# A decode attention kernel: transposing half a K tile per instruction, and setup work moved off VectorE

## The chip, the cores and the metric

The kernel runs on one core of a Trainium2 chip. A core has a matrix engine (TensorE, PE in the profile), three engines for elementwise work (VectorE or DVE, ScalarE or ACT, GpSimd or POOL), an engine that issues loads (SyncE or SP) and 16 load engines (DMA) that bring data from memory (HBM) to the on-chip buffer (SBUF). TensorE writes to a second buffer, PSUM. The engines run beside each other and wait for one another through semaphores.

The metric is the time on the device in microseconds (us), as the median of several runs. The profile shows one execution; its span is a little shorter than the time.

## What is computed

For four sequences with one new token each, the kernel adds three things: the input `x`, an attention over a cache, and an MLP mixer. Cut to what matters:

```python
def _A_ref(x, k_cache, v_cache, wq, wo):          # attention over the last W = 2048 positions
    q = (x @ wq).reshape(B, 1, 32, 128)           # 32 query heads, 16 key/value heads
    k = repeat(k_cache[:, :, Sk - W:, :], 2)      # (4, 16, 2048, 128) of K are read, bf16
    v = repeat(v_cache[:, :, Sk - W:, :], 2)      # and as much of V
    p = softmax(q @ k.T * 128 ** -0.5)
    return (p @ v).reshape(B, 1, 4096) @ wo

def _B_ref(x, w1, w2, w3, w4):                    # with one token the first mixing part is zero
    ...
    x1 = x + hs
    return x1 + gelu(layernorm(x1) @ w3) @ w4     # w3: 576 x 4608, w4: 4608 x 576

xn = layernorm(x)
out = x + _A_ref(xn, ...) + _B_ref(xn, ...)
```

Nearly all of the 87 MB that the kernel has to read is K and V: 16 heads, each with 2 MB of K and 2 MB of V for the four sequences. The weights wq, w3, w4 and wo make up the rest. Each value is used for one token only, so there is little arithmetic for each byte.

## The kernel before

The kernel goes through the 16 key/value heads in 16 steps. Step `t` makes the scores of head `t`; beside that, it does the softmax of head `t - 1`, the product with V ("PV") of head `t - 2`, and the rest of heads `t - 3` and `t - 4`. A step has four slices.

K lies in SBUF with positions on the partitions, and the scores need it with the head's 128 dimensions there. VectorE transposes it in blocks of 32 x 32, a quarter of a K tile for each instruction, through a pool of three buffers:

```python
ktp = ctx.enter_context(tc.tile_pool(name="kt", bufs=3))
...
def k_transpose(h, s):
    src = kv_tiles["K", h][:].bitcast(I32)[:, s * SC:(s + 1) * SC, :].rearrange("p c (ib i) -> p ib c i", i=QD)
    kt = ktp.tile([P, 2, SC, QD], I32, tag="kt")
    nc.vector.transpose(out=kt[:], in_=src)
    kts[h, s] = kt

def k_scores(h, s):                    # TensorE: four matmuls for a slice
    kt = kts.pop((h, s))[:].bitcast(BF16)
    for ie in range(4):
        ...
        nc.tensor.matmul(out=S_ps[h][:], lhsT=qz[:, z0:z0 + P], rhs=kt[...], ...)

def sm_max(h):                         # VectorE: the maxima of a head's scores
    nc.vector.reduce_max(out=mx[:], in_=S_ps[h][:], axis=AX.X)
    nc.vector.tensor_scalar(out=dm[:], in0=sel_g[:], scalar1=mx[:, 0:1], ...)

def pv(h, s):                          # TensorE: four matmuls for a slice
    for g in range(NQD):
        c = s * NQD + g
        nc.tensor.matmul(out=O_ps[h][g * QD:(g + 1) * QD], lhsT=PT[h][:, c, :], rhs=vn[:, :, c, :], ...)
```

The helper `part` cuts small tiles from the first buffer of the wo pool. The loop over the steps, in which the order of the instructions is fixed by hand:

```python
k_transpose(0, 0)
for t in range(Hkv):
    hm, hv, hf, hp = t - 1, t - 2, t - 3, t - 4
    for s in range(NSL):                       # NSL = 4
        if s == NSL - 1 and hm >= 0:
            sm_turn(hm)                        # VectorE: transpose of the exponentials
        n = t * NSL + s + 1
        if n < Hkv * NSL:
            k_transpose(*divmod(n, NSL))       # the quarter for the slice that follows
        if s == 0:
            if hm >= 0:
                sm_max(hm)
            if hv >= 0:
                sm_rec(hv)                     # VectorE: reciprocal of the denominator
            if hp >= 0:
                o_pick(hp)                     # VectorE, every fourth head
            if hf >= 0:
                o_scale(hf)                    # ScalarE
            k_mask(t)                          # TensorE
        elif s == 1 and hm >= 0:
            sm_maxT(hm)                        # TensorE
        elif s == 2:
            if hm >= 0:
                sm_sub(hm)                     # TensorE: subtracts the maxima
                sm_exp(hm)                     # ScalarE
            if hf >= 0:
                o_sum(hf)                      # VectorE
        elif s == 3 and hm >= 0:
            sm_den(hm)                         # TensorE
        k_scores(t, s)
        if hv >= 0 and s > 0:
            pv(hv, s - 1)
            if s == NSL - 1:
                pv(hv, s)
        if s == 1:
            ...                                # sm_neg(hm) on VectorE, o_turn(hf), o_proj(hp) on TensorE
        ...                                    # o_spread; in step 7 the MLP: mlp_g, mlp_turn, mlp_act
    pos["free"] += 1                           # the K tile of this step
    if hv >= 0:
        pos["free"] += 1                       # the V tile of head t - 2
    flush_loads()
```

`flush_loads` issues the next loads on one queue, in the order K0, K1, K2, V0, K3, V1, K4, V2 (then w3), K5, V3 and so on, with a piece of wo ahead of V0, V4, V8 and V12, and w4 in six pieces at the end. K and V tiles share six buffers of 2 MB. A load waits until its buffer is free. After the loop, the last two heads are finished, and then TensorE multiplies the MLP's activations with w4, piece by piece, and head 15's last part with wo. The result is the sum of two accumulators in PSUM.

Ahead of the loop stands a setup: two layernorms, selection matrices made from an identity, and the projection with wq. In it, and in the MLP's activation, VectorE does these operations which the change touches:

```python
nc.vector.memset(dup[:], 0.0)                                  # in transposed(), called twice
nc.vector.tensor_copy(out=dup[:, e, e:P:2], in_=...)           # two per call
nc.vector.tensor_copy(out=sel[:, :, :, kb, :], in_=...)        # four
nc.vector.tensor_copy(out=ohT[:], in_=oh_ps[:, 0, :])
nc.vector.tensor_copy(out=sel_jb[:], in_=sel_j[:])
nc.vector.tensor_copy(out=j_row[:], in_=jT_ps[:])
nc.vector.tensor_copy(out=same_j[:]..., in_=...)
nc.vector.tensor_tensor(out=xsum[:], in0=xn_f[:], in1=x_bf[:], op=ALU.add)

def mlp_act():                                                 # once, 128 x 144 values
    nc.vector.tensor_tensor(out=u[:], in0=xs[:], in1=xs[:], op=ALU.mult)
    nc.vector.tensor_scalar(out=u[:], in0=u[:], scalar1=GELU_A, scalar2=1.0, ...)
    nc.vector.tensor_tensor(out=u[:], in0=u[:], in1=xs[:], op=ALU.mult)
    nc.scalar.activation(out=u[:], in_=u[:], func=ACT.Tanh, scale=GELU_C)
    nc.vector.tensor_scalar(out=u[:], in0=u[:], scalar1=0.5, scalar2=0.5, ...)
    nc.vector.tensor_tensor(out=gT[:, :, ROWS], in0=u[:], in1=xs[:], op=ALU.mult)
```

Of the kernel before, what the change touches and what calls it, by code (L numbers as in the profile page):

```python
# [8 lines left out]
ACT = mybir.ActivationFunctionType  # L9
ALU = mybir.AluOpType  # L10
AX = mybir.AxisListType
BF16 = mybir.dt.bfloat16
F32 = mybir.dt.float32
I32 = mybir.dt.int32
# [8 lines left out]
def kernel(  # L23
# [14 lines left out]
    nc = tc.nc  # L38
    P = 128
    B, Sq, D = A_x.shape  # L40
    _, Hkv, Sk, Dh = A_k_cache.shape
# [5 lines left out]
    KJ = 4  # L47
# [5 lines left out]
    NJ = B * rep  # L53
    QD = 32
    NQD = P // QD
    NSL = 4
    SC = NC // NSL
# [7 lines left out]
    GELU_A = 0.044715  # L65
# [11 lines left out]
    kvp = ctx.enter_context(tc.tile_pool(name="kv", bufs=NKV))  # L77
    wp = ctx.enter_context(tc.tile_pool(name="w", bufs=1))
    wop = ctx.enter_context(tc.tile_pool(name="wo", bufs=2))
    ktp = ctx.enter_context(tc.tile_pool(name="kt", bufs=3))  # L80
    ptp = ctx.enter_context(tc.tile_pool(name="pt", bufs=2))
    bigp = ctx.enter_context(tc.tile_pool(name="big", bufs=2))
    const = ctx.enter_context(tc.tile_pool(name="const", bufs=1))
# [9 lines left out]
    kv_tiles = {}  # L93
# [22 lines left out]
    x_bf = part(D, B)  # L116
# [52 lines left out]
    ROWS = slice(NI - 1, NI - 1 + OR, NI)  # L169
    gT = cleared([P, NF, OW], "gT")  # L170
    op = cleared([P, WOR, OW], "op")
# [30 lines left out]

    def transposed(src_bf, T):
        dup = small.tile([B, 2, P], BF16, tag="dup")
        nc.vector.memset(dup[:], 0.0)
        for e in range(2):
            nc.vector.tensor_copy(out=dup[:, e, e:P:2], in_=src_bf[:, KJ * P:D])
        tp = ps_m.tile([P, KJ + 2, B], BF16, tag="m", name="tp")
        for j in range(KJ):
            nc.tensor.transpose(out=tp[:, j, :], in_=src_bf[:, j:KJ * P:KJ], identity=ident_bf[0:B, 0:B])  # L210
        for e in range(2):
            nc.tensor.transpose(out=tp[:, KJ + e, :], in_=dup[:, e, :], identity=ident_bf[0:B, 0:B])
        nc.vector.tensor_copy(out=T[:, :, 0:B], in_=tp[:])

    xn_f = part(2 * D, B).bitcast(F32)
# [3 lines left out]

    kts = {}  # L220

    def k_transpose(h, s):
        src = kv_tiles["K", h][:].bitcast(I32)[:, s * SC:(s + 1) * SC, :].rearrange("p c (ib i) -> p ib c i", i=QD)
        kt = ktp.tile([P, 2, SC, QD], I32, tag="kt")
        nc.vector.transpose(out=kt[:], in_=src)  # L225
        kts[h, s] = kt


    sel = part(4 * P).rearrange("p (i e k x) -> p i e k x", i=2, e=2, k=NQD)
    for kb in range(NQD):  # L230
        nc.vector.tensor_copy(out=sel[:, :, :, kb, :],
                              in_=ident_bf[:].rearrange("p (ib i e) -> p ib e i", ib=2, e=2))
    oh4 = const.tile([P, B], F32)
    nc.vector.reduce_sum(out=oh4[:], in_=ident_f[:].rearrange("p (k b r) -> p b k r", b=B, r=rep), axis=AX.XY)
# [2 lines left out]
    oh_ps = ps_m.tile([B, 2, P], F32, tag="m", name="oh_ps")  # L237
    nc.tensor.transpose(out=oh_ps[:, 0, :], in_=oh4[:], identity=ident_f[:])
    nc.tensor.transpose(out=oh_ps[:, 1, :], in_=ohk[:], identity=ident_f[:])
    ohT = const.tile([B, P], BF16)  # L240
    nc.vector.tensor_copy(out=ohT[:], in_=oh_ps[:, 0, :])
    negbig = const.tile([B, QD], BF16)
    nc.vector.tensor_scalar(out=negbig[:], in0=oh_ps[:, 1, 0:QD], scalar1=-1.0, scalar2=BIG,
                            op0=ALU.add, op1=ALU.mult)

    NG = P // NJ
    sel_j = const.tile([P, NJ], F32)
    nc.vector.reduce_sum(out=sel_j[:], in_=ident_f[:].rearrange("p (g j) -> p j g", j=NJ), axis=AX.X)
    sel_jb = const.tile([P, NJ], BF16)
    nc.vector.tensor_copy(out=sel_jb[:], in_=sel_j[:])  # L250
    sel_g = const.tile([P, NG], BF16)
    with nc.allow_low_precision("zeros and ones"):
        nc.vector.reduce_sum(out=sel_g[:], in_=ident_f[:].rearrange("p (g j) -> p g j", j=NJ), axis=AX.X)
    jT_ps = ps_m.tile([NJ, P], F32, tag="m", name="jT_ps")
    nc.tensor.transpose(out=jT_ps[:], in_=sel_j[:], identity=ident_f[:])
    j_row = const.tile([NJ, P], BF16)
    nc.vector.tensor_copy(out=j_row[:], in_=jT_ps[:])
    same_j = const.tile([P, P], F32)
    nc.vector.tensor_copy(out=same_j[:].rearrange("p (g j) -> p g j", j=NJ),
                          in_=sel_j[:].unsqueeze(1).to_broadcast([P, NG, NJ]))  # L260


# [7 lines left out]
    nc.gpsimd.memset(idz[:], 0.0)  # L270
    nc.gpsimd.tensor_copy(out=idz[:, ROWS], in_=ident_f[0:B, 0:B])
    xsum = xn_f
    nc.vector.tensor_tensor(out=xsum[:], in0=xn_f[:], in1=x_bf[:], op=ALU.add)
    acc_matmuls([(idz[:], xsum)])
    ln2_bf = part(D, B)
    layernorm(None, ln2_bf, xn_bf)
# [25 lines left out]
    for r in range(2):  # L302
        nc.vector.tensor_copy(out=q_bf[:, r],
                              in_=qT_ps[:, r].rearrange("p u (g x) -> p g u x", g=NQD)[:, :, :, 0:B])
    qs_ps = ps_m.tile([P, Hkv, 4, rep, B], F32, tag="m", name="qs_ps")
    for ie in range(4):
        ib, e = divmod(ie, 2)
# [13 lines left out]
    E = {}  # L321
# [5 lines left out]
    def k_mask(h):  # L327
        S_ps[h] = ps_s.tile([P, NW], F32, tag="S", name="S")
        nc.tensor.matmul(out=S_ps[h][:].rearrange("p (c k) -> p c k", k=QD), lhsT=ohT[:],  # L329
                         rhs=negbig[:].unsqueeze(1).to_broadcast([B, SC, QD]),  # L330
                         start=True, stop=False, skip_group_check=True)

    def k_scores(h, s):
        kt = kts.pop((h, s))[:].bitcast(BF16)
        for ie in range(4):
            ib, e = divmod(ie, 2)
            z0 = (h * 4 + ie) * P + ZP - s * NJ
            nc.tensor.matmul(out=S_ps[h][:], lhsT=qz[:, z0:z0 + P],  # L338
                             rhs=kt[:, ib, :, e:2 * QD:2].rearrange("p c k -> p (c k)"),
                             start=False, stop=False, skip_group_check=True)  # L340

    def sm_max(h):
# [18 lines left out]
                         start=False, stop=False, skip_group_check=True)  # L361

    def sm_exp(h):
        E[h] = ptp.tile([P, SC, QD], BF16, tag="e", name="E")
        rs = small.tile([P, 1], F32, tag="rs", bufs=3)
        nc.scalar.activation(out=E[h][:].rearrange("p c k -> p (c k)"), in_=S_ps.pop(h)[:], func=ACT.Exp, scale=scale,  # L366
                             accum_out=rs[:])
        st["rs", h] = rs
# [5 lines left out]
    def sm_den(h):  # L374
        dn = ps_m.tile([P, 1], F32, tag="m", name="dn")
        nc.tensor.matmul(out=dn[:], lhsT=same_j[:], rhs=st.pop(("rs", h))[:], start=True, stop=True)  # L376
        st["dn", h] = dn
# [6 lines left out]
    def pv(h, s):  # L384
        if s == 0:
            O_ps[h] = ps_o.tile([P, NSL, Dh], F32, tag="O", name="O")
        vn = kv_tiles["V", h][:].rearrange("p (s c) d -> p s c d", s=NSL)
        for g in range(NQD):
            c = s * NQD + g
            nc.tensor.matmul(out=O_ps[h][g * QD:(g + 1) * QD], lhsT=PT[h][:, c, :], rhs=vn[:, :, c, :],  # L390
                             start=(s == 0), stop=False, skip_group_check=True)
        if s == NSL - 1:
            PT.pop(h)

    def o_scale(h):
        O_sb[h] = bigp.tile([P, NSL, Dh], F32, tag="big", name="O_sb")
        nc.scalar.activation(out=O_sb[h][:], in_=O_ps.pop(h)[:], func=ACT.Copy, scale=st.pop(("rd", h))[:, 0:1])  # L397
# [77 lines left out]

    def mlp_act():
        u = const.tile([P, NF, B], F32, name="g_u")
        nc.vector.tensor_tensor(out=u[:], in0=xs[:], in1=xs[:], op=ALU.mult)
        nc.vector.tensor_scalar(out=u[:], in0=u[:], scalar1=GELU_A, scalar2=1.0, op0=ALU.mult, op1=ALU.add)
        nc.vector.tensor_tensor(out=u[:], in0=u[:], in1=xs[:], op=ALU.mult)  # L480
        nc.scalar.activation(out=u[:], in_=u[:], func=ACT.Tanh, scale=GELU_C)
        nc.vector.tensor_scalar(out=u[:], in0=u[:], scalar1=0.5, scalar2=0.5, op0=ALU.mult, op1=ALU.add)
        nc.vector.tensor_tensor(out=gT[:, :, ROWS], in0=u[:], in1=xs[:], op=ALU.mult)

    def mlp_out(lo, hi):
        w4 = w_tiles["w4"]
# [29 lines left out]
    for t in range(Hkv):  # L516
        hm, hv, hf, hp = t - 1, t - 2, t - 3, t - 4
        for s in range(NSL):
            if s == NSL - 1 and hm >= 0:
                sm_turn(hm)  # L520
            n = t * NSL + s + 1
            if n < Hkv * NSL:
                k_transpose(*divmod(n, NSL))

            if s == 0:
                if hm >= 0:
                    sm_max(hm)
                if hv >= 0:
                    sm_rec(hv)
                if hp >= 0:  # L530
                    o_pick(hp)
                if hf >= 0:
                    o_scale(hf)
                k_mask(t)
            elif s == 1 and hm >= 0:
                sm_maxT(hm)
            elif s == 2:
                if hm >= 0:
                    sm_sub(hm)
                    sm_exp(hm)  # L540
                if hf >= 0:
                    o_sum(hf)
            elif s == 3 and hm >= 0:
                sm_den(hm)
            k_scores(t, s)
            if hv >= 0 and s > 0:
                pv(hv, s - 1)
                if s == NSL - 1:
                    pv(hv, s)
            if s == 1:  # L550
                if hm >= 0:
                    sm_neg(hm)
                if hf >= 0:
                    o_turn(hf)
                if hp >= 0:
                    o_proj(hp)
            elif s == 3 and hf >= 0:
                o_spread(hf)
            if t == G_AT:
                if s < 3:  # L560
                    mlp_g(s)
                if s > 0:
                    mlp_turn(s - 1)
                if s == NSL - 1:
                    mlp_act()
        pos["free"] += 1
        if hv >= 0:
            pos["free"] += 1
        flush_loads()
# [77 lines left out]
```

## Time and profile before

| what | value |
|---|---|
| time, median of 3 runs | 212.51 us (212.32 to 212.71) |
| span of the profiled execution | 210.7 us |
| bytes read | 87.17 MB on the queue that loads K, V and the weights |
| K transposes on VectorE | 64, 1222 ns each |
| score matmuls on TensorE (`S<-kt,qz`) | 75.1 us busy in all |
| PV matmuls on TensorE (`O<-vn,PT`) | 24.0 us busy in all |
| mean clock granted to TensorE | 0.87 of full speed |

In a page of the profile, the busy time of an engine stands first, then its share of the span and its number of instructions. A row of digits cuts the span into 40 equal slices; a 9 means busy for 90% or more. A group of instructions is given as line, engine, operation, what it writes and reads, and its count; then the busy time and the mean of one in ns; then the engine's idle time just before such instructions, and what ended most of it. In a timeline a line starts with the start and the duration in us; in brackets is the idle time before it with its releaser. The load share of a stretch is the mean busy share of the 16 load engines, and can come out slightly over 1.

### The profile page before, as it was taken

Reading aid. Unit: us, or ns where it says so; the run is one execution under the profiler, and the core shown is the slowest. Engines: PE = TensorE matmul, PEld = TensorE weight load, DVE = VectorE, ACT = ScalarE, POOL = GpSimd, SP = SyncE. Lnnn points to the kernel's source line nnn. Section 1 sums busy time; section 2 is a strip of 40 time slices with the busy share of each in tenths; the row PEclk is TensorE's granted clock in tenths of the full one; section 3 lists DMA queues with packets and bytes.
Section 4 is the critical chain, followed back from the end, with each engine's and each line's share of the span. In section 5 each row is a group of like instructions: output and inputs, shape, how many; then the busy total and the mean of one; then the engine's idle time right before and its main releaser. Section 6 shows DMA issues by size and latency. Waiting matters only on the chain.

```text
span 210.7 us, 2383 instructions
## 1 busy us (share of the span) xinstructions
PE 153.2 (73%) x941; PEld 61.2 (29%) x955; DVE 120.7 (57%) x217; ACT 33.9 (16%) x64; POOL 2.7 (1%) x15
## 2 busy tenths in 40 slices
PE   0288399768660069559997699999885757999585
PEld 0133133223220013123443224334332212343253
DVE  3741889794910094917227867985939481845300
ACT  7602201112020001111122012121120201113200
POOL 4010000000000000000000000000000000000000
PEclk9999669999995558966999759999999965599969
DMA  7999999999999999999999999999999999999990
GB/s 299 398 426 423 439 426 417 428 445 417 487 388 411 447 426 420 429 442 439 414 439 435 417 432 429 442 426 428 428 432 429 422 440 432 423 432 447 397 396 31
DMA packets 6659, 87.32 MB, mean 414 GB/s; under 512 B 748, under 2 KB 1016, under 8 KB 1656
## 3 DMA queue, kind: packets, MB, share of 16 engines
q1 hardware_dynamic: 6640, 87.17, 97.1%
q8 instruction: 7, 0.11, 0.2%
q10 hardware_dynamic: 8, 0.00, 0.1%
q14 instruction: 4, 0.03, 0.0%
HBM read 87.17 MB, written 0.00 MB: 414 GB/s over the span
## 4 chain that ended last, share of the span: by engine, by line
DMA 63%; PE 26%; DVE 7%; issue 2%; ACT 1%; SPq 0%; DVEq 0%
DMA vn<-in_A_v_cache_dram 29%; DMA w_sb<-in_B_w_dram 16%; DMA kn<-in_A_k_cache_dram 12%; PE S L338 8%; DMA wq_sb<-in_A_wq_dram 6%; PE acc L183 4%; DVE kt L225 4%; PE O L390 3%; PE oT L403 2%; PE g_ps L456 2%; PE q_ps L285 2%; PE S L360 1%; PE dn L376 1%; DVE qz L317 1%; PE gT_ps L468 1%
## 5 line engine op out<-in xcount | busy, mean ns | idle before, releaser
L338 PE MATMUL S<-kt,qz 128*128 128x512 bf16 x242 | 75.1, 432 | 24.8 <-DVE kt L225 22.3
L225 DVE STREAM_TRANSPOSE kt<-kn 128x1024 int32<-128x1024 int32 x64 | 76.6, 1222 | 25.7 <-DMA kn<-in_A_k_cache_dram 23.8
L338 PEld LDWEIGHTS <-qz 128*128 128x128 bf16 x256 | 23.7, 109 | 54.9 <-issue 38.5
L390 PE MATMUL O<-vn,PT 128*32 128x512 bf16 x256 | 24.0, 417 | 7.4 <-DMA vn<-in_A_v_cache_dram 7.1
L366 ACT ACTIVATE E<-S 128x512 bf16<-128x512 f32 x16 | 9.5, 597 | 97.4 <-PE S L360 97.4
L372 DVE STREAM_TRANSPOSE PT<-E 128x512 bf16<-128x512 bf16 x16 | 11.4, 710 | 14.0 <-ACT E L366 13.9
L397 ACT ACTIVATE O_sb<-O,rd 128x512 f32<-128x512 f32 x16 | 11.0, 686 | 39.4 <-issue 28.9
L390 PEld LDWEIGHTS <-PT 128*32 128x32 bf16 x256 | 5.9, 95 | 29.6 <-issue 28.9
L413 DVE TENSOR_REDUCE on<-oT 128x8 bf16<-128x128 f32 x16 | 4.5, 283 | 14.4 <-PE oT L403 14.4
L403 PE MATMUL oT<-ident_w,O_sb 128*128 128x128 f32 x64 | 12.4, 324 | 0.3 <-ACT O_sb L397 0.3
L344 DVE TENSOR_REDUCE mx<-S 128x1 f32<-128x512 f32 x16 | 10.6, 660 | 2.0 <-PE S L338 2.0
L351 PE MATMUL mg<-dm,sel_jb 128*8 128x16 bf16 x16 | 2.8, 173 | 9.2 <-DVE dm L346 9.1
L403 PEld LDWEIGHTS oT<-ident_w,O_sb 128*128 128x128 f32 x64 | 7.9, 160 | 5.0 <-issue 4.5
L183 PE MATMUL acc<-w_sb,gT 128*8 128x288 bf16 x38 | 6.6, 342 | 2.4 <-DMA w_sb<-in_B_w_dram 2.4
L183 PE MATMUL acc<-wo_sb,op 128*8 128x288 bf16 x56 | 7.5, 286 | 0.0
L360 PE MATMUL S<-nm,j_row 8*128 8x512 bf16 x16 | 6.9, 429 | 0.0
L376 PEld LDWEIGHTS dn<-rs,same_j 128*128 128x128 f32 x32 | 5.4, 212 | 4.3 <-issue 3.6
L376 PE MATMUL dn<-rs,same_j 128*128 128x1 f32 x32 | 6.6, 275 | 0.0
L329 PE MATMUL S<-negbig,ohT 4*128 4x512 bf16 x16 | 6.4, 399 | 0.0
L183 PE MATMUL acc_odd<-w_sb,gT 128*8 128x288 bf16 x34 | 6.1, 349 | 0.0
L351 PEld LDWEIGHTS <-sel_jb 128*8 128x8 bf16 x16 | 1.3, 83 | 15.3 <-DVE dm L346 12.9
L183 PEld LDWEIGHTS <-gT 128*8 128x8 bf16 x72 | 4.1, 103 | 4.6 <-issue 2.4
(93 smaller groups left out, 80.0 us busy)
## 6 DMA issues: line engine op xcount, KB each, us to landing
kn<-in_A_k_cache_dram SPq DMA_DIRECT2D x16, 2048.0 KB, 23.5
vn<-in_A_v_cache_dram SPq DMA_DIRECT2D x16, 2048.0 KB, 25.9
wo_sb<-in_A_wo_dram SPq DMA_DIRECT2D x4, 1152.0 KB, 25.6
w_sb<-in_B_w_dram SPq DMA_DIRECT2D x1, 4608.0 KB, 33.4
wq_sb<-in_A_wq_dram SPq DMA_DIRECT2D x1, 4096.0 KB, 12.7
w_sb<-in_B_w_dram SPq DMA_DIRECT2D x1, 2592.0 KB, 33.1
w_sb<-in_B_w_dram SPq DMA_DIRECT2D x2, 864.0 KB, 34.5
w_sb<-in_B_w_dram SPq DMA_DIRECT2D x2, 576.0 KB, 32.6
```

What stands on the lines that cost most here:

```text
L183: nc.tensor.matmul(out=to[q:q + OR, :], lhsT=lhsT[:, NI - 1 - i:NI - 1 - i + OR], rhs=rhs[:, i * CW:(i + 1) * CW], start=start, stop=False ...
L225: nc.vector.transpose(out=kt[:], in_=src)
L329: nc.tensor.matmul(out=S_ps[h][:].rearrange("p (c k) -> p c k", k=QD), lhsT=ohT[:], rhs=negbig[:].unsqueeze(1).to_broadcast([B, SC, QD]), ...
L338: nc.tensor.matmul(out=S_ps[h][:], lhsT=qz[:, z0:z0 + P], rhs=kt[:, ib, :, e:2 * QD:2].rearrange("p c k -> p (c k)"), start=False, stop=Fa ...
L344: nc.vector.reduce_max(out=mx[:], in_=S_ps[h][:], axis=AX.X)
L360: nc.tensor.matmul(out=S_ps[h][:], lhsT=j_row[:], rhs=st.pop(("nm", h))[:, 0:1].to_broadcast([NJ, NW]), start=False, stop=False, skip_grou ...
L366: nc.scalar.activation(out=E[h][:].rearrange("p c k -> p (c k)"), in_=S_ps.pop(h)[:], func=ACT.Exp, scale=scale, accum_out=rs[:])
L372: nc.vector.transpose(out=PT[h][:], in_=E.pop(h)[:])
L376: nc.tensor.matmul(out=dn[:], lhsT=same_j[:], rhs=st.pop(("rs", h))[:], start=True, stop=True)
L390: nc.tensor.matmul(out=O_ps[h][g * QD:(g + 1) * QD], lhsT=PT[h][:, c, :], rhs=vn[:, :, c, :], start=(s == 0), stop=False, skip_group_check ...
L397: nc.scalar.activation(out=O_sb[h][:], in_=O_ps.pop(h)[:], func=ACT.Copy, scale=st.pop(("rd", h))[:, 0:1])
L403: nc.tensor.transpose(out=oT[:, s, :], in_=o[:, s, :], identity=ident_w[:, s * NJ:s * NJ + P])
```

## The change

The change transposes half a K tile with one instruction, into two buffers of twice the size. The first half of the next head is transposed in the last slice of a step, the second half in the first slice of its own step, behind the maxima of the head before it. PV stands ahead of the scores in each slice. Selection copies, an addition and the MLP's activation go from VectorE to GpSimd, and two copies to ScalarE. The pool of the exponentials (`E`) has one buffer in place of two. It is meant to give VectorE less to do, and to let the maxima, on which the softmax waits, go ahead of a transpose. The order of the loads is not touched. The core of the diff:

```diff
-    ktp = ctx.enter_context(tc.tile_pool(name="kt", bufs=3))
+    ktp = ctx.enter_context(tc.tile_pool(name="kt", bufs=2))
...
-        nc.vector.memset(dup[:], 0.0)
+        nc.gpsimd.memset(dup[:], 0.0)
         for e in range(2):
-            nc.vector.tensor_copy(out=dup[:, e, e:P:2], in_=src_bf[:, KJ * P:D])
+            nc.gpsimd.tensor_copy(out=dup[:, e, e:P:2], in_=src_bf[:, KJ * P:D])
...
-    def k_transpose(h, s):
-        src = kv_tiles["K", h][:].bitcast(I32)[:, s * SC:(s + 1) * SC, :].rearrange("p c (ib i) -> p ib c i", i=QD)
-        kt = ktp.tile([P, 2, SC, QD], I32, tag="kt")
+    def k_transpose(h, half):
+        c0 = half * 2 * SC
+        src = kv_tiles["K", h][:].bitcast(I32)[:, c0:c0 + 2 * SC, :].rearrange("p c (ib i) -> p ib c i", i=QD)
+        kt = ktp.tile([P, 2, 2 * SC, QD], I32, tag="kt")
         nc.vector.transpose(out=kt[:], in_=src)
...
-        nc.vector.tensor_copy(out=sel[:, :, :, kb, :],
+        nc.gpsimd.tensor_copy(out=sel[:, :, :, kb, :],
...
-    nc.vector.tensor_copy(out=ohT[:], in_=oh_ps[:, 0, :])
+    nc.scalar.activation(out=ohT[:], in_=oh_ps[:, 0, :], func=ACT.Copy)
...
(likewise: sel_jb and same_j to GpSimd, j_row to ScalarE)
...
-    nc.vector.tensor_tensor(out=xsum[:], in0=xn_f[:], in1=x_bf[:], op=ALU.add)
+    nc.gpsimd.tensor_tensor(out=xsum[:], in0=xn_f[:], in1=x_bf[:], op=ALU.add)
...
-        E[h] = ptp.tile([P, SC, QD], BF16, tag="e", name="E")
+        E[h] = ptp.tile([P, SC, QD], BF16, tag="e", name="E", bufs=1)
...
(in mlp_act, the five nc.vector operations become nc.gpsimd operations)
...
-            n = t * NSL + s + 1
-            if n < Hkv * NSL:
-                k_transpose(*divmod(n, NSL))
+            if s == NSL - 1 and t + 1 < Hkv:
+                k_transpose(t + 1, 0)
 
             if s == 0:
                 if hm >= 0:
                     sm_max(hm)
                 ...
                 if hf >= 0:
                     o_scale(hf)
+                k_transpose(t, 1)
                 k_mask(t)
...
+            if hv >= 0:
+                pv(hv, s)
             k_scores(t, s)
-            if hv >= 0 and s > 0:
-                pv(hv, s - 1)
-                if s == NSL - 1:
-                    pv(hv, s)
```

More of the change, by code (lines that the diff above doesn't have):

```diff
@@ L220 @@
     kts = {}
-    def k_transpose(h, s):
-        src = kv_tiles["K", h][:].bitcast(I32)[:, s * SC:(s + 1) * SC, :].rearrange("p c (ib i) -> p ib c i", i=QD)
-        kt = ktp.tile([P, 2, SC, QD], I32, tag="kt")
+    def k_transpose(h, half):
+        c0 = half * 2 * SC
+        src = kv_tiles["K", h][:].bitcast(I32)[:, c0:c0 + 2 * SC, :].rearrange("p c (ib i) -> p ib c i", i=QD)
+        kt = ktp.tile([P, 2, 2 * SC, QD], I32, tag="kt")
         nc.vector.transpose(out=kt[:], in_=src)
-        kts[h, s] = kt
+        kts[h, half] = kt
     sel = part(4 * P).rearrange("p (i e k x) -> p i e k x", i=2, e=2, k=NQD)
     for kb in range(NQD):
-        nc.vector.tensor_copy(out=sel[:, :, :, kb, :],
+        nc.gpsimd.tensor_copy(out=sel[:, :, :, kb, :],
                               in_=ident_bf[:].rearrange("p (ib i e) -> p ib e i", ib=2, e=2))
@@ L249 @@
     sel_jb = const.tile([P, NJ], BF16)
-    nc.vector.tensor_copy(out=sel_jb[:], in_=sel_j[:])
+    nc.gpsimd.tensor_copy(out=sel_jb[:], in_=sel_j[:])
     sel_g = const.tile([P, NG], BF16)
@@ L256 @@
     j_row = const.tile([NJ, P], BF16)
-    nc.vector.tensor_copy(out=j_row[:], in_=jT_ps[:])
+    nc.scalar.activation(out=j_row[:], in_=jT_ps[:], func=ACT.Copy)
     same_j = const.tile([P, P], F32)
-    nc.vector.tensor_copy(out=same_j[:].rearrange("p (g j) -> p g j", j=NJ),
+    nc.gpsimd.tensor_copy(out=same_j[:].rearrange("p (g j) -> p g j", j=NJ),
                           in_=sel_j[:].unsqueeze(1).to_broadcast([P, NG, NJ]))
@@ L333, in k_scores @@
     def k_scores(h, s):
-        kt = kts.pop((h, s))[:].bitcast(BF16)
+        half, c0 = s // 2, s % 2 * SC
+        kt = kts[h, half][:].bitcast(BF16)
+        if s % 2:
+            kts.pop((h, half))
         for ie in range(4):
@@ L338, in k_scores @@
             nc.tensor.matmul(out=S_ps[h][:], lhsT=qz[:, z0:z0 + P],
-                             rhs=kt[:, ib, :, e:2 * QD:2].rearrange("p c k -> p (c k)"),
+                             rhs=kt[:, ib, c0:c0 + SC, e:2 * QD:2].rearrange("p c k -> p (c k)"),
                              start=False, stop=False, skip_group_check=True)
@@ L477, in mlp_act @@
         u = const.tile([P, NF, B], F32, name="g_u")
-        nc.vector.tensor_tensor(out=u[:], in0=xs[:], in1=xs[:], op=ALU.mult)
-        nc.vector.tensor_scalar(out=u[:], in0=u[:], scalar1=GELU_A, scalar2=1.0, op0=ALU.mult, op1=ALU.add)
-        nc.vector.tensor_tensor(out=u[:], in0=u[:], in1=xs[:], op=ALU.mult)
+        nc.gpsimd.tensor_tensor(out=u[:], in0=xs[:], in1=xs[:], op=ALU.mult)
+        nc.gpsimd.tensor_scalar(out=u[:], in0=u[:], scalar1=GELU_A, scalar2=1.0, op0=ALU.mult, op1=ALU.add)
+        nc.gpsimd.tensor_tensor(out=u[:], in0=u[:], in1=xs[:], op=ALU.mult)
         nc.scalar.activation(out=u[:], in_=u[:], func=ACT.Tanh, scale=GELU_C)
-        nc.vector.tensor_scalar(out=u[:], in0=u[:], scalar1=0.5, scalar2=0.5, op0=ALU.mult, op1=ALU.add)
-        nc.vector.tensor_tensor(out=gT[:, :, ROWS], in0=u[:], in1=xs[:], op=ALU.mult)
+        nc.gpsimd.tensor_scalar(out=u[:], in0=u[:], scalar1=0.5, scalar2=0.5, op0=ALU.mult, op1=ALU.add)
+        nc.gpsimd.tensor_tensor(out=gT[:, :, ROWS], in0=u[:], in1=xs[:], op=ALU.mult)
     def mlp_out(lo, hi):
```

## The prediction

> **What bounds the kernel now.** I read in this order: the page's busy shares with the 40 slices, the stretch from 30 to 200 us, the queue that issues the loads, the chain that ended last, and the instructions around the last loads.
>
> ```profile
> PE 153.2 (73%) x941; PEld 61.2 (29%) x955; DVE 120.7 (57%) x217; ACT 33.9 (16%) x64; POOL 2.7 (1%) x15
> DMA  7999999999999999999999999999999999999990
> q1 hardware_dynamic: 6640, 87.17, 97.1%
> DMA 63%; PE 26%; DVE 7%; issue 2%; ACT 1%; SPq 0%; DVEq 0%
> ...
> L225 DVE STREAM_TRANSPOSE kt<-kn 128x1024 int32<-128x1024 int32 x64 | 76.6, 1222 | 25.7 <-DMA kn<-in_A_k_cache_dram 23.8
> ```
>
> No engine is full: VectorE is busy for 57% of the span, TensorE for 73%. The load engines are: 97.1% of the whole span on one queue, and all slices but the first and last at nine tenths. VectorE's costliest line, the K transpose, waits 23.8 us for K loads: it waits for data, not data for it.
>
> ```profile
> core 0: us, PE busy (x) PEld busy (x) DVE busy (x) ACT busy (x) POOL busy (x), PEclk, DMA share, GB/s
> 30.00:200.00 170.00, 129.63 (x769) 50.27 (x781) 103.66 (x171) 23.67 (x52) 0.00 (x0) 0.87 1.01 430
> ```
>
> Between 30 and 200 us the loads run at 430 GB/s with a share of 1.01, so without a gap. The 87.17 MB at 430 GB/s are 202.7 us. What is left of the 210.7 us span, 8 us, is the slow start and the end. Whether compute could starve the loads is seen in the queue (start, duration, what is issued):
>
> ```profile
> 27.38 0.54 SPq L103 DMA_DIRECT2D kn<-in_A_k_cache_dram  x1
> ...
> 109.48 0.54 SPq L103 DMA_DIRECT2D kn<-in_A_k_cache_dram  x1
> ...
> 153.42 0.53 SPq L103 DMA_DIRECT2D kn<-in_A_k_cache_dram  x1
> 157.17 10.34 SPq L103 DMA_DIRECT2D vn<-in_A_v_cache_dram  x3
> 167.57 17.36 SPq L141 DMA_DIRECT2D w_sb<-in_B_w_dram  x6
> ```
>
> K and V loads are issued when a buffer comes free, but land 16.0 to 41.1 us later (the answer for the load line), because four or five 2 MB tiles stand ahead of them. A buffer must come free some 16 us late before a load engine runs dry. From 157 us on even the issuing waits for the queue: nothing in the last 50 us depends on a buffer. Last, the end:
>
> ```profile
> 174.92 0.62 PE L390 MATMUL O<-vn,PT 128*32 128x512 bf16 x4 [2.33 <-DMA vn<-in_A_v_cache_dram]
> ...
> 179.75 2.37 DVE L225 STREAM_TRANSPOSE kt<-kn 128x1024 int32<-128x1024 int32 x2 [1.10 <-DMA kn<-in_A_k_cache_dram]
> ...
> 200.72 0.40 PE L183 MATMUL acc<-w_sb,gT 128*8 128x288 bf16 x1 [2.45 <-DMA w_sb<-in_B_w_dram]
> ...
> 207.43 0.65 PE L183 MATMUL acc<-w_sb,gT 128*8 128x288 bf16 x4
> 207.64 0.40 ACT L608 ACTIVATE odd<-acc_odd 8x288 f32<-8x288 f32 x1 [10.82 <-PE acc_odd L183]
> 208.61 0.36 SPq L616 DMA_DIRECT2D out_dram<-fin  x1
> ```
>
> All attention is done at 198.3 us; TensorE stands idle for 2.45 us until the first piece of w4 lands at 200.7, then does 88 matmuls in pairs (72 with w4, 16 with the last wo), and ends at about 207.6. The first pairs start 0.24 us apart, those after 204.0 0.12 us: after the idle stretch the granted clock was 0.50 from 201 to 203 and 1.00 from 204 on.
>
> **What the Trainium skill says.** "DMA: Bandwidth & Descriptors", section "Where 436 GB/s comes from", puts the ceiling of a core's load engines at 435 GB/s; the 430 GB/s measured here is within about 1% of it, so the stream has nothing to gain from better overlap. "TensorE: Matmul & The Clock Gate", section "What's actually happening", says the array falls to half clock after an idle window of about 3.4 us and comes back after a busy one, with windows that run freely; the trace agrees in kind (2.45 us idle, then 3.3 us at half clock). "Vector Engine (DVE) Microarchitecture Reference", section "3.8 The reshape front-end and per-opcode configuration", gives one element per cycle and lane for the transpose; the trace agrees, with 1222 ns for 1024 elements and 710 ns for 512, so 1.0 ns an element. "GPSIMD Engine Reference", section "3.1 Elementwise — side-by-side cycle accounting", has GpSimd nearly twice as slow as VectorE on two-input elementwise work; the kernel before has no such operation of any size on GpSimd, so no run here shows it yet.
>
> **The change part by part.**
>
> *Half a tile per transpose.* 64 transposes of 1024 elements become 32 of 2048. By the slope of 1.0 ns, one takes 1222 + 1024 = 2250 ns, an estimate. Two of the old ones back to back take 2.37 us (179.75). So 0.12 us is saved per pair, 32 x 0.12 = 3.8 us of VectorE in the whole kernel. It lies beside waits for data: 0 on the path.
>
> *The order on VectorE.* Before, the second quarter of a K tile is transposed ahead of the maxima of the head before (2.37 us, then the maximum at 182.04). After, the first half is, then the maxima, then the second half. In a step that waits for K the maximum follows 2.25 us after landing instead of 2.37: no difference. In a step that doesn't wait, the maximum no longer stands behind a transpose of its own step, but the transpose just ahead is the longer one. VectorE's chain per step is then 0.65 + 0.23 + 0.16 (maximum, product, reciprocal) + 2.25 + 0.12 + 0.29 + 0.71 + 2.25 = 6.7 us, and about 1.2 us of waiting for the subtraction and the exponential: 8 us. That is what a step takes now where data do not hold it (K issues at 129.06, 136.90 and 144.78, 7.9 us apart). Loads bring a step, 4.19 MB, in 9.75 us. Compute keeps its lead.
>
> *When K buffers come free.* Before, the last quarter is transposed in the third slice of the step; after, the second half at its head. In a step bound by data this comes to the same: at the step whose K tile landed at 167.33 the last quarter was done at 172.95, and 167.33 + 2.25 + 1.04 + 2.25 is 172.9. In other steps it is somewhat earlier. A load that lands 16 us or more after its issue does not land sooner for that: 0.
>
> *PV ahead of the scores.* Before, the score matmuls of two slices run ahead of the first PV group. After, PV comes first, and the V tile it needs lands right behind this step's K tile (with wo3 between at 167 to 175 us). So in a step bound by data TensorE does nothing until V lands. Before, it had done two score groups by then: 2 x 1.07 us at full clock, or 2 x 1.89. That work moves behind V: 2 to 4 us later per such step, not accumulating, as each step is tied to its own V. In exchange TensorE then works through without a second wait and warms up once.
>
> *The end.* V of head 12 lands at 174.9. Step 14's work on TensorE is about 8 us at full clock, 9.7 to 11.4 us if the first 3.4 to 6.8 us are at half clock: it ends at 184.6 to 186.3. V of head 13 is there by 184.6. Step 15 has another 2.1 us of wo matmuls: 10.1 us, ending at 194.7 to 196.4, where it now ends at 192.3. What stands between that and the w4 matmuls took 198.3 - 192.3 = 6.0 us: attention ends at 200.7 to 202.4, where it now ends at 198.3. So the idle 2.45 us are used up and perhaps 1.7 us more. But TensorE comes to w4 warm: 44 pairs x 0.12 = 5.3 us, instead of 6.9 us with the slow start. That ends at 206.0 to 207.7. The last w4 pieces cannot land much before 206.5, as after 205 only 197 and then 27 GB/s still came in. So: 206.5 to 207.7 against 207.6, a change of -1.1 to +0.1 us, and some risk of +1 or 2 us if step 14 or 15 takes longer.
>
> *Setup off VectorE.* It loses about 3.6 us of copies and an addition (4 x 0.22, 4 x 0.19, 2 x 0.17, 0.28 + 0.17 + 0.28 + 0.20 + 0.74). The projection starts at 13.97 us, when wq lands; VectorE's last setup copy is at 13.84. GpSimd gets 0.2 us copies and one addition of 576 elements, 0.74 us on VectorE and some 1.4 us at twice that: an estimate. The second layernorm waits for GpSimd's power behind them, which should still be ready before 12 us. The bound is wq's landing: 0.
>
> *The MLP activation.* 0.31 + 0.23 + 0.31 + 0.24 + 0.36 = 1.45 us leave VectorE once, about 2 us with the wait for Tanh. On GpSimd it takes perhaps 3 us; ScalarE's next scaling waits behind Tanh for 1 to 2 us. It is needed only for w4, 85 us later: 0.
>
> Sum: the stream 0, the start 0, the end -1.1 to +0.1 us with a tail upward: 212.4 us.
>
> **The rivals.** First, VectorE was the bound and the change makes the kernel faster by some of the 3.8 + 5 us it takes off it, to about 205 us. For it: the line with the largest idle time on TensorE's score matmuls ends at the transpose (22.3 us). Against: those transposes themselves waited 23.8 us for K loads, and the load share is 1.01. I give it little. Second, the wait for V takes the place of the wait for K, TensorE is cold in every step, attention ends at 204 us or later and w4 follows: 212 + 2 to 4 us. For it: half clock from 170 to 183.5 us now, in just such a step. Against: what delays TensorE also removes its idle gap, and a busy TensorE is at full clock. Third, GpSimd is so slow in the setup that the projection starts late: even 5 us late, the loads have enough buffers until 27.4 us and beyond, and the lag is caught up: within 1 us. Fourth, the buffers come free too late and the queue runs dry: needs 16 us of lag; hardly.
>
> **Range and chances.** The stream sets 202.7 us of it whichever way the engines go. Faster by over 2% needs 208.3 us, less than the loads allow with their start and end: 0.02. Slower by over 2% needs 216.8, the second rival at its worst: 0.04. The range is the end's: down 1.2 us, up 1.6 us.
>
> **What would show it.** Right: load share 1.0 and about 430 GB/s from 30 to 200 us; K transposes x32 near 2250 ns; loads that land 16 us and more after their issue, as before; PV, no longer the transposes, as TensorE's waiter, on V loads; w4's first matmul at 200.7 to 202.4 with less idle time before it and closer pairs. Wrong: slices with a load share under nine tenths in the middle, a transpose far from 2250 ns, or w4's first matmul after 203 us.

## The result, and the profile after

The kernel after takes 211.66 us (median of 6 runs, 211.45 to 212.13); the kernel before, measured beside it, takes 212.65 us. The ratio is 0.9948, with a 95% interval from 0.9924 to 0.9972. The change gains about 1 us, half a percent. The span of the profiled execution fell from 210.7 to 209.6 us.

First the page of the kernel after: the busy shares, the load share by slices, the load queue, and three groups of instructions (busy us, mean ns, then the idle time before them and what ended it).

```profile
PE 145.8 (70%) x941; PEld 62.6 (30%) x955; DVE 113.6 (54%) x165; ACT 34.4 (16%) x66; POOL 8.9 (4%) x33
DMA  7999999999999999999999999999999999999992
q1 hardware_dynamic: 6640, 87.17, 97.6%
...
L342 PE MATMUL S<-kt,qz 128*128 128x512 bf16 x242 | 75.4, 435 | 7.2 <-DVE kt L226 4.8
L226 DVE STREAM_TRANSPOSE kt<-kn 128x2048 int32<-128x2048 int32 x32 | 73.0, 2285 | 13.5 <-DMA kn<-in_A_k_cache_dram 12.1
L394 PE MATMUL O<-vn,PT 128*32 128x512 bf16 x256 | 27.2, 425 | 38.8 <-DMA vn<-in_A_v_cache_dram 36.2
```

The two groups of TensorE were these in the kernel before:

```profile
L338 PE MATMUL S<-kt,qz 128*128 128x512 bf16 x242 | 75.1, 432 | 24.8 <-DVE kt L225 22.3
L390 PE MATMUL O<-vn,PT 128*32 128x512 bf16 x256 | 24.0, 417 | 7.4 <-DMA vn<-in_A_v_cache_dram 7.1
```

VectorE has less to do, and the loads are as full as they were. TensorE's idle time has moved from the score matmuls, which stood behind the K transposes (22.3 us, now 4.8), to PV, which stands behind the V loads (7.1 us, now 36.2). So the large waits changed their name and their place, and the time hardly changed. The stretch from 30 to 200 us of the kernel after shows why:

```profile
core 0: us, PE busy (x) PEld busy (x) DVE busy (x) ACT busy (x) POOL busy (x), PEclk, DMA share, GB/s
30.00:200.00 170.00, 124.43 (x757) 52.40 (x770) 98.51 (x134) 23.67 (x52) 2.03 (x5) 0.87 1.01 430
```

The load share and the 430 GB/s are those of before. Where the microsecond came from is seen in the timeline of the end of the kernel after (start, duration, instruction, idle time before it):

```profile
200.77 0.35 PE L426 MATMUL R<-on,sel_wo 128*128 128x32 bf16 x8 [0.38 <-DVE on L417]
201.05 0.29 PE L183 MATMUL acc<-w_sb,gT 128*8 128x288 bf16 x1
201.05 0.29 PE L183 MATMUL acc_odd<-w_sb,gT 128*8 128x288 bf16 x1
201.18 0.29 PE L183 MATMUL acc<-w_sb,gT 128*8 128x288 bf16 x1
...
206.37 0.66 PE L183 MATMUL acc<-w_sb,gT 128*8 128x288 bf16 x4
...
207.55 0.36 SPq L618 DMA_DIRECT2D out_dram<-fin  x1
```

Attention ends at 201.1 us, 2.8 us later than before. Right behind it come the w4 matmuls, with no idle time, and the pairs are 0.12 us apart from the first. They start 0.3 us later than before and end earlier: the result is sent off at 207.55 us instead of 208.61. From 202 to 204 us the granted clock (third number from the end of the line) was 0.51 before and is 1.00 after:

```profile
202.00:204.00 2.00, 2.00 (x20) 1.12 (x18) 0.00 (x0) 0.00 (x0) 0.00 (x0) 0.51 1.02 425
```
```profile
202.00:204.00 2.00, 2.00 (x38) 1.45 (x35) 0.04 (x1) 0.00 (x0) 0.00 (x0) 1.00 0.97 394
```

### The profile page after: what moved, and what is told of

The parts are those of the page before. It is cut to its first block, busy times and chain, and to the rows that moved or that the text cites. A ratio compares the mean times of both kernels' runs of the same rounds, so it can differ in the third digit from the quotient of the medians.

```text
span 209.6 us, 2332 instructions
## 1 busy us (share of the span) xinstructions
PE 145.8 (70%) x941; PEld 62.6 (30%) x955; DVE 113.6 (54%) x165; ACT 34.4 (16%) x66; POOL 8.9 (4%) x33
## 4 chain that ended last, share of the span: by engine, by line
DMA 60%; PE 26%; DVE 9%; ACT 2%; issue 1%; SPq 0%; DVEq 0%; ACTq 0%
DMA vn<-in_A_v_cache_dram 38%; DMA w_sb<-in_B_w_dram 16%; PE S L342 9%; DMA wq_sb<-in_A_wq_dram 6%; PE acc L183 5%; DVE kt L226 5%; PE O L394 3%; PE g_ps L460 2%; PE q_ps L286 2%; PE oT L407 2%; DVE mx L348 1%; DVE PT L376 1%; PE S L364 1%; DVE qz L318 1%; PE gT_ps L472 1%
## 5 line engine op out<-in xcount | busy, mean ns | idle before, releaser
L226 DVE STREAM_TRANSPOSE kt<-kn 128x2048 int32<-128x2048 int32 x32 | 73.0, 2285 | 13.5 <-DMA kn<-in_A_k_cache_dram 12.1
L394 PE MATMUL O<-vn,PT 128*32 128x512 bf16 x256 | 27.2, 425 | 38.8 <-DMA vn<-in_A_v_cache_dram 36.2
L342 PEld LDWEIGHTS <-qz 128*128 128x128 bf16 x256 | 21.9, 104 | 44.2 <-issue 28.1
L394 PEld LDWEIGHTS <-PT 128*32 128x32 bf16 x256 | 7.3, 95 | 48.2 <-issue 41.0
L407 PE MATMUL oT<-ident_w,O_sb 128*128 128x128 f32 x64 | 10.8, 295 | 0.4 <-ACT O_sb L401 0.3
L360 DVE TENSOR_REDUCE nm<-mg 8x1 bf16<-8x16 f32 x16 | 2.3, 141 | 11.4 <-PE mg L355 11.4
L286 PE MATMUL q_ps<-wq_sb,xnT 128*32 128x512 bf16 x40 | 4.2, 596 | 1.8 <-DMA wq_sb<-in_A_wq_dram 1.8
L183 PEld LDWEIGHTS <-op 128*8 128x8 bf16 x64 | 4.7, 87 | 2.2 <-issue 0.3
L183 PE MATMUL acc<-w_sb,gT 128*8 128x288 bf16 x38 | 5.1, 286 | 0.0
L460 PE MATMUL g_ps<-w_sb,ln2T 128*32 128x512 bf16 (+1 forms) x50 | 4.9, 445 | 0.0
## 6 DMA issues: line engine op xcount, KB each, us to landing
kn<-in_A_k_cache_dram SPq DMA_DIRECT2D x16, 2048.0 KB, 22.8
vn<-in_A_v_cache_dram SPq DMA_DIRECT2D x16, 2048.0 KB, 24.8
```

Source lines behind the costliest of these rows:

```text
L183: nc.tensor.matmul(out=to[q:q + OR, :], lhsT=lhsT[:, NI - 1 - i:NI - 1 - i + OR], rhs=rhs[:, i * CW:(i + 1) * CW], start=start, stop=False ...
L286: nc.tensor.matmul(out=q_ps[r][g * QD:(g + 1) * QD, :], lhsT=xnT[:, k, :], rhs=wq_sb[:, col:col + NW], start=(j == 0), stop=False, skip_gr ...
L407: nc.tensor.transpose(out=oT[:, s, :], in_=o[:, s, :], identity=ident_w[:, s * NJ:s * NJ + P])
L460: nc.tensor.matmul(out=g_ps[g * QD:(g + 1) * QD], lhsT=ln2T[:, k, :], rhs=rhs, start=(j == 0), stop=False, skip_group_check=True)
```

## The experiments

The theory to be tested: all of the gain lies at the end. PV ahead of the scores holds TensorE back by the waits for V; it finishes attention about when w4 lands, has little or no idle time there, and comes to w4 warm (at full clock) and not cold (at half clock). Two rivals: the gain comes from VectorE's lighter load (A), or from the setup that moved to GpSimd (B). Each ratio below is against runs of the kernel before that were made beside that experiment (medians 212.48 to 212.74 us).

### One part alone: PV ahead of the scores

The kernel before, with this part of the change:

```diff
+            if hv >= 0:
+                pv(hv, s)
             k_scores(t, s)
-            if hv >= 0 and s > 0:
-                pv(hv, s - 1)
-                if s == NSL - 1:
-                    pv(hv, s)
```

> The kernel before with one part of the change: PV ahead of the scores in each slice; quarter transposes, and all setup and activation work where it was. Theory (the gain is at the end: TensorE, held back by the waits for V, finishes attention when w4's first piece lands at about 200.7 us and does not idle and cool before it): about 1.0 us faster than before, 211.6 us; first w4 matmul at 200.7 to 201.5 with under 1 us of idle time before it and pairs 0.12 us apart. Rival A (the gain comes from VectorE, relieved of 5 us and of half the transposes): no change, 212.5 us. Rival B (it comes from the start, where setup moved to GpSimd): no change.

Measured: 211.60 us, ratio 0.9952 (0.9933 to 0.9971). This part alone gives the whole gain. The end in its timeline:

```profile
199.25 0.35 PE L422 MATMUL R<-on,sel_wo 128*128 128x32 bf16 x8 [0.38 <-DVE on L413]
200.41 0.28 PE L183 MATMUL acc<-w_sb,gT 128*8 128x288 bf16 x1 [0.80 <-DMA w_sb<-in_B_w_dram]
...
200.53 0.28 PE L183 MATMUL acc<-w_sb,gT 128*8 128x288 bf16 x1
```

Attention ends at 199.6 us, only 1.3 us later than before. TensorE does idle for 0.80 us, and the pairs are 0.12 us apart all the same; so it is in the two kernels below that keep PV first and six pieces of w4 (half the transposes: 0.80 us, five buffers: 0.76 us). The gap of 2.45 us had to become shorter, not to vanish.

### All but that part

The kernel after, with the order of PV and scores put back (the diff above in reverse).

> The kernel after with only the order of PV and scores put back; half-tile transposes, moved setup and moved activation stay. Theory: the gain goes, 212.4 to 212.8 us; attention ends some 2 us before w4's first piece lands, TensorE idles over 2 us and the first w4 pairs are 0.24 us apart for about 3 us. Rivals A and B: it stays at 211.6 us.

Measured: 212.49 us, ratio 0.9997 (0.9978 to 1.0016). Half-tile transposes, setup on GpSimd and ScalarE, the moved activation and the single buffer of `E` are together worth nothing that can be measured. Rivals A and B fall. The end in its timeline:

```profile
197.28 0.35 PE L426 MATMUL R<-on,sel_wo 128*128 128x32 bf16 x8 [0.38 <-DVE on L417]
200.74 0.40 PE L183 MATMUL acc<-w_sb,gT 128*8 128x288 bf16 x1 [3.10 <-DMA w_sb<-in_B_w_dram]
...
200.93 0.44 PE L183 MATMUL acc<-w_sb,gT 128*8 128x288 bf16 x1
...
201.17 0.44 PE L183 MATMUL acc<-w_sb,gT 128*8 128x288 bf16 x1
```

Attention ends earlier than in any kernel so far, TensorE idles 3.10 us, and the pairs are 0.24 us apart. In this execution they stayed so until about 205 us, and it took 213.3 us; most others of this kernel took 212.3 to 212.6. How long the slow stretch lasts varies. The times of the kernel before fall into two groups as well (beside the experiments, 53 of 97 executions took under 212.8 us, the others 212.9 to 213.9), so the gain is some 0.8 us against the one and 1.7 us against the other. That a longer half clock makes the second group is likely, but not shown for that kernel: its profile is one of the first.

### Nothing of the change, but a busy TensorE

If the clock is the cause, useless work in the gap must bring the gain. The kernel before, with eleven matmuls whose result nothing uses:

```diff
     o_pick(hl)
+    filler = ps_m.tile([P, NW], F32, tag="m", name="filler")
+    for _ in range(11):
+        nc.tensor.matmul(out=filler[:], lhsT=ident_bf[:],
+                         rhs=sel_wo[:].rearrange("p i h d -> p (i h d)")[:, 0:NW], start=True, stop=True)
     mlp_out(*pieces[0])
```

> The kernel before, with nothing of the change: eleven matmuls of 128x512 into an unused PSUM tile stand between the last wo selection and the w4 matmuls, about 2.4 us at full clock, to fill the idle time there. Their result is used by nothing. Theory (it is the clock at w4's start that makes the 1 us): 211.6 us, as fast as the kernel after, although TensorE does more work; w4 pairs 0.12 us apart from the first. If the end came from something else in the order (which head is finished when, the wo part), it stays at 212.5 us or is slower by up to what the fillers delay w4.

Measured: 211.55 us (211.52 to 211.64), ratio 0.9950 (0.9932 to 0.9969). The end in its timeline:

```profile
197.64 2.53 PE L603 MATMUL filler<-sel_wo,ident_bf 128*128 128x512 bf16 x10
200.67 0.28 PE L183 MATMUL acc<-w_sb,gT 128*8 128x288 bf16 x1 [0.50 <-DMA w_sb<-in_B_w_dram]
...
200.79 0.28 PE L183 MATMUL acc<-w_sb,gT 128*8 128x288 bf16 x1
```

w4 starts at 200.67 us, as it does before (200.72). What differs is the pace: 0.12 us from pair to pair instead of 0.24. (The record has ten of the eleven fillers.) With 2.5 us of wasted work the kernel before becomes as fast as the kernel after. So the half clock at w4's start is worth the whole microsecond.

### How late may w4 start?

The same with 22 fillers in place of 11.

> The kernel before with 22 fillers instead of 11, so about 4.8 us at full clock from about 197.6 to 198.3 us on: w4's matmuls start at about 202.4 to 203 us, some 2 us after their first piece landed. Theory: 44 pairs at 0.12 us take 5.3 us from there, so the end comes at 207.7 to 208.3 instead of 207.6 us: 212.5 to 213.3 us. So a start 2 us late with a warm array costs about what a timely start with a cold one does. If w4's matmuls had room to spare against the landing of the last pieces, it would stay at 211.6.

Measured: 212.94 us, ratio 1.0001 (0.9985 to 1.0017). In its timeline the fillers last until 203.0 us:

```profile
198.19 4.91 PE L603 MATMUL filler<-sel_wo,ident_bf 128*128 128x512 bf16 x22
203.02 0.29 PE L183 MATMUL acc<-w_sb,gT 128*8 128x288 bf16 x1
...
209.35 0.37 SPq L620 DMA_DIRECT2D out_dram<-fin  x1
```

A warm start 2.3 us late gives the whole gain back: it costs what a timely start at half clock costs. So attention may end later than w4's landing by a little, not by 2 us.

### Does VectorE matter at all?

The kernel after with half of its K transposes left out; all four score slices use the first half of the tile.

```diff
-        half, c0 = s // 2, s % 2 * SC
+        half, c0 = 0, s % 2 * SC
...
-                k_transpose(t, 1)
```

> The kernel after with only the first half of each K tile transposed, and all four score slices made from that half: 16 of the 32 transposes are left out, 36 us of VectorE's work. All loads are still made and TensorE's matmuls are the same in number and shape. Theory (the stream of loads sets the time up to the end): 211.7 us, within 0.6. Rival A (VectorE bounds the loop): faster by up to a good part of 36 us, at least below 208.

Measured: 211.57 us, ratio 0.9948 (0.9929 to 0.9966). The transposes and the stretch from 30 to 200 us in its profile:

```profile
L226 DVE STREAM_TRANSPOSE kt<-kn 128x2048 int32<-128x2048 int32 x16 | 36.4, 2277 | 12.5 <-DMA kn<-in_A_k_cache_dram 12.4
```
```profile
30.00:200.00 170.00, 127.08 (x770) 53.48 (x782) 66.70 (x120) 23.69 (x52) 2.04 (x5) 0.86 1.01 431
```

VectorE loses 36 us of work against the kernel after, and the time stays where it is.

### Do the loads need their lead?

The kernel after with five K and V buffers (`NKV = 5`) in place of six.

> The kernel after with five K and V buffers instead of six, all else the same. Loads are issued about one tile, 4.9 us, later against the data. If the lead of 19 us and more between issue and landing is room to spare, as the prediction took it: landing times fall by some 5 us, the load share stays at 1.01 between 30 and 200 us, and the time stays at 211.7 us within 0.6. If the lead is needed: gaps in the stream and 2 us or more on top.

Measured: 211.57 us, ratio 0.9940 (0.9916 to 0.9964). The landing times of its K and of its V loads:

```profile
DMA to landing us min/median/max: 11.6/19.5/32.3
```
```profile
DMA to landing us min/median/max: 13.2/19.9/32.3
```

Medians of 22.8 and 24.8 us in the kernel after fall by 3.3 and 4.9 us, and the load share between 30 and 200 us stays at 1.01. The lead is room to spare. 2 MB of SBUF stand free for other use.

### Is anything left at the end?

In the kernel after, the load share sinks to about 0.4 in the last microsecond of loading. The first try was to load w4 in four pieces instead of six:

```diff
-    W4_PIECES = [0, NFH, NF - 12, NF - 6, NF - 2, NF - 1, NF]
+    W4_PIECES = [0, NFH, NF - 6, NF - 2, NF]
...
-    mlp_out(*pieces[3])
...
-    for lo, hi in pieces[4:]:
+    for lo, hi in pieces[3:]:
```

> The kernel after with w4 loaded in four pieces instead of six (rows 0, 18, 30, 34 to 36 of 36 per partition), to ask whether anything is left at the end. In the kernel after the load share falls to about 0.4 in the last microsecond of loading, which the many small pieces may cause. If they do: 0.2 to 0.6 us faster than after, 211.1 to 211.4 us. If the last landing is set by the bytes and the engines' own spread: 211.6 us or slightly slower, as the last step waits for two rows at once.

Measured: 212.33 us, ratio 0.9986 (0.9973 to 0.9999): 0.7 us slower than after, against both expectations. The profiled execution, which took 212.97 us, shows a half clock after an idle time of only 0.75 us:

```profile
200.54 0.28 PE L183 MATMUL acc<-w_sb,gT 128*8 128x288 bf16 x1 [0.75 <-DMA w_sb<-in_B_w_dram]
...
200.66 0.40 PE L183 MATMUL acc<-w_sb,gT 128*8 128x288 bf16 x1
...
200.86 0.45 PE L183 MATMUL acc<-w_sb,gT 128*8 128x288 bf16 x1
```

This execution is 0.6 us above the median, so its half clock explains at most this execution. At first I took it for the cause, and put four fillers ahead of w4, with four pieces and with six.

> The kernel with four pieces of w4, plus four fillers (128x512 matmuls into an unused PSUM tile, 0.9 us at full clock) between the last wo selection and the w4 matmuls. It asks why four pieces gave 212.33 us. If the half clock did it (the pairs were 0.24 us apart until about 204 us although TensorE had idled only 0.75 us): 211.4 to 211.7 us, pairs 0.12 us apart from the first. If larger pieces themselves cost the time: it stays near 212.3 us.

> The kernel after with the same four fillers and its six pieces: whether a warm start made certain beats the kernel after. In the executions of the kernel after the times go from 211.45 to 212.13 us; if the slower ones are those in which the clock fell before w4, the fillers make all of them about 211.5 us: median 211.5 to 211.6 and a spread under 0.3 us. If w4 then starts later because of the fillers: up to 0.3 us slower.

Measured: with four pieces 212.39 us, ratio 0.9985 (0.9968 to 1.0001), so not cured; with six 211.72 us (211.45 to 212.23), ratio 0.9955 (0.9937 to 0.9972), no better than after and with no smaller spread. With four pieces and fillers the w4 pairs are 0.12 us apart from the first, in an execution of 212.38 us: the clock at w4 is not what makes four pieces slow. Nor is it shown to make the spread of the kernel after. The last run settled the first of the two: eleven fillers, which had given the steadiest times, with four pieces.

> The kernel before with eleven fillers, as in the run at 211.55 us, but with w4 in four pieces. With four pieces the kernel after was at 212.3 to 212.4 us, with and without four fillers, and each time the profile shows half clock in some stretch of the last 15 us. Here TensorE is warm up to w4's start. If the pieces are innocent and the clock did it: 211.4 to 211.7 us. If four pieces cost the time by themselves (a first wo or w4 matmul that waits longer for a landing): 212.0 us or more, with TensorE waiting for w4 between the pieces.

Measured: 212.41 us, ratio 0.9986 (0.9971 to 1.0002). The w4 pairs are 0.12 us apart throughout. The answer lies behind the last matmul. First the sending of the result and SyncE's wait for the store in this run, then the same two lines of the run with eleven fillers and six pieces (the wait's columns: total, times, longest):

```profile
207.84 0.37 SPq L619 DMA_DIRECT2D out_dram<-fin  x1
```
```profile
SPq L645 <- DMA out_dram<-fin: 0.7, 1, 0.7
```
```profile
207.76 0.37 SPq L620 DMA_DIRECT2D out_dram<-fin  x1
```
```profile
SPq L646 <- DMA out_dram<-fin: 0.2, 1, 0.2
```

Both kernels send the result off within 0.1 us of each other. With four pieces the store takes longer: the span ends at 210.6 us, 2.8 us after the issue, and with six at 209.9, 2.1 us after it. The two other runs with four pieces show the same (2.7 us). TensorE waited 0.77 us for the second piece, as the second expectation had it, but made that up: the issue of the result shows it. Why the store of 4.5 KB takes 0.6 us longer when four loads precede it was not tried; SyncE had then waited for 28 us instead of 18.

No version beat the kernel after by more than its own spread. The kernel with one part of the change, the kernel with eleven fillers, the one with half the transposes and the one with five buffers all lie between 211.55 and 211.60 us.

## Why the prediction was right

*The stream sets the time.* Right: 430 GB/s and a share of 1.01, before and after; leaving out 36 us of VectorE's work and taking away a buffer each left the time as it was. K and V loads landed 17.1 us and more after their issue, as foretold. (K and V are 67 of the 87 MB, so three quarters, not nearly all.)

*Half a tile per transpose.* Foretold 2250 ns, measured 2285; it was worth 0, as foretold, together with the rest of the work taken off VectorE (the run with PV behind the scores).

*Setup and activation on GpSimd.* The addition took 1.26 us, 1.7 times as long as on VectorE (estimate 1.4 us), the five operations of the activation 2.0 us in all, and 2.7 us with the waits (some 3 foretold). The copy that closes the second layernorm was done at 12.4 us, ahead of wq's landing at 13.9, where the projection starts as before. 0, as foretold.

*PV ahead of the scores.* Right in kind: waits for V took the place of waits for K. The sum was right by luck: attention was said to end at 200.7 to 202.4 us and ended at 201.1, but two errors cancel. The work of steps 14 and 15 was set too high, at 8 and 10.1 us at full clock. Step 14 was done at 182.7 us, not at 184.6 to 186.3; with its 3.3 us at half clock taken at half, its work is 6.2 us, an estimate. Step 15 waited for its V until 184.5 in any case; then a second stretch at half clock, to about 188.3 us, which the prediction did not have, made it 9.9 us long. In these lines of its timeline four score matmuls take 1.88 us, where they take 1.08 us at full clock:

```profile
184.53 0.40 PE L394 MATMUL O<-vn,PT 128*32 128x512 bf16 x4 [1.50 <-DMA vn<-in_A_v_cache_dram]
...
184.86 1.88 PE L342 MATMUL S<-kt,qz 128*128 128x512 bf16 x4
```

With PV alone, with five buffers, and with four fillers ahead of six pieces, step 14 was at half clock for 5.0 to 6.1 us, as foretold (3.4 to 6.8). It was done by 184.0 us, step 15 took 8.4 us without such a stretch, and attention ended at 199.6 to 199.7 us, earlier than the range. Nor do the traces bear out that a busy TensorE is at full clock: in the kernel before it worked almost without a pause from 174.9 to 183.5 us, at half clock.

*The end.* The range of -1.1 to +0.1 us for the issue of the result holds the measured -1.06, and the two terms behind it, the shorter idle gap and the warm pairs, are what the runs with one part alone and with fillers show. What was off is the weight: 212.4 us took a late w4 start to be likely as well as an early one, plus a tail upward, so the measured change lies near the lower end of the range. In the kernels that come to w4 warm and in time, the landing of w4's fourth piece (rows 30 to 33) sets the end. With eleven fillers, and likewise with PV alone, half the transposes or five buffers, TensorE waits 0.5 us for it:

```profile
206.09 0.28 PE L183 MATMUL acc<-w_sb,gT 128*8 128x288 bf16 x1 [0.49 <-DMA w_sb<-in_B_w_dram]
```

The last matmuls follow without a further wait, at 206.4 to 206.6 us; that is the floor of 206.5 named in the prediction, which put it down to the last pieces. In the kernel after the pairs run on to this point, with one step of 0.29 us in place of 0.12 at 205.88 us: it came to w4 with less than 0.2 us to spare.

*The rivals.* VectorE as the bound and the GpSimd setup fell to two runs. The second rival (a cold TensorE in every step and a late end) did not come about, but the run with 22 fillers shows that it was a real danger: 2 us of lateness take the gain back.

## What to carry to other kernels

When the loads run without a gap, look at the last transfers and what follows them; here 36 us of VectorE's work could be left out without a trace in the time. A matrix engine that finishes early and waits for the last weights can be slower over all than one that arrives just in time, because it then works at half clock; an order that keeps it busy up to that point, or a few matmuls for nothing, was worth the whole gain here. To tell parts of a change from each other, undo one and do one alone: here one moved line carried everything.

## What was not expected of the hardware

The granted clock does not follow the last idle gap alone. TensorE idled 0.80 us ahead of w4 and stayed at full clock in the run with PV alone; in the run with four pieces it idled 0.75 us and fell to half clock 0.1 us after it had started again. In the kernel after it idled 1.50 us ahead of step 15 and fell 0.4 us after the start; in the kernel before, after 2.45 us, the clock likewise fell only as the matmuls began. The Trainium skill's page "TensorE: Matmul & The Clock Gate", section "What's actually happening", has windows of about 3.4 us that run freely, which would fit; no run here shows the windows themselves. An idle time of that length, which the prediction took from there, was not needed.

A store of 4.5 KB took 2.1 us from its issue to the end of the span in all kernels with six pieces of w4 and 2.7 to 2.8 us in the three with four pieces. The spread of the kernel after (211.45 to 212.13 us, against 211.52 to 211.64 with eleven fillers) stays unexplained.
